# Moving the query and key transposes of three of sixteen head pairs of a routed-attention kernel from TensorE to VectorE, with earlier weights and a new plan for the placing DMAs

## The chip, the cores and the metric

The kernel runs on one core of one Trainium2 chip. The metric is the device time of one execution in microseconds (us). The profile is one execution, taken by the hardware profiler. PE is TensorE, PEld its weight loads, DVE is VectorE, ACT is ScalarE, POOL is GpSimd and SP is SyncE, which here does nothing but issue DMAs. Executions come with a state. Only fast ones are compared, unless a sentence says otherwise.

## The reference, cut to what matters

```python
q_n, k_n, c_n = (each row divided by its norm)          # shortened
q_assign = argmax(einsum('bhsd,hcd->bhsc', q_n, c_n))   # 16 clusters per head
k_assign = argmax(einsum('bhsd,hcd->bhsc', k_n, c_n))
mask = q_assign[..., :, None] == k_assign[..., None, :]
attn = softmax(where(mask, q @ k.T / 8, -1e9))          # 4 x 8 heads, 768 x 768
x = (attn @ v) laid out as 3072 tokens x 512
h = x @ w_in                                            # 512 x 2048
g = h + sin(alpha * h)**2 / (alpha + 1e-9)
out = g @ w_out                                         # 2048 x 512
```

The batch has four members. For each of them the kernel runs an attention stage (8 heads as 4 *pairs*, 12 *steps* for a pair, 48 in all) and then a feed-forward stage, FF. Pairs are numbered 0 to 15 and steps 0 to 191. One step computes a 128x768 block of scores on TensorE, its exponential on ScalarE, and six value products on TensorE for an earlier block.

## The kernel before: the parts that the change touches

A pair's q and k come in with positions on the partitions and must be turned, so that the head dimension lies there. The kernel has two ways for it. By TensorE, three 128x128 transposes into PSUM and a copy make one of four groups:

```python
def prep_T(m, g, bk=None, eng="dve"):
    ...
    for jj in range(NJ2):
        nc.tensor.transpose(out=bk[:, P*jj : P*jj + P], in_=src[:, h, P*jj : P*jj + P], identity=ident_f)
    nc.vector.tensor_scalar_mul(out=s["T32"][:, g, :], in0=bk[:, 0:HS], scalar1=1.0 / QDIV)
```

By VectorE, a transpose within 32x32 blocks goes to `Tq`, and eight DMAs on SP then put the blocks in their places in `T32`:

```python
def prep_D(m, g):
    ...
    nc.vector.transpose(out=s["Tq"][:, g, :], in_=src[:, h, :].rearrange("p (j e d) -> p e j d", e=2, d=32))

def prep_S(m):                       # "the placing"
    s["T32"] = trp.tile([P, 4, HS], F32, tag="T32", name="T32")
    for i in range(4):
        for e in range(2):
            lo = D * (i // 2) + 32 * e
            nc.sync.dma_start(out=s["T32"][lo : lo + 32, :, QS*(i%2) : QS*(i%2) + QS],
                              in_=s["Tq"][32*i : 32*i + 32, :, QS*e : QS*e + QS])
```

From `T32` come three things: casts on POOL into `QK`, the operand of the scores; the *cluster products* (`prep_asn`, four matmuls against the centroids); and from these, by four VectorE pieces (`prep_hot`), one-hot *rows* that four more DMAs on SP carry into `QK` (`prep_move`), where they mask the scores. TensorE takes its instructions in order, so a cluster product whose `T32` is not there holds back the scores of every later step.

Before, pairs 2 to 7 went by TensorE and pairs 8 to 15 by VectorE. A dictionary of steps says when each piece is put into its engine's order:

```python
first = {1: 0, 2: 4, 3: 12, 4: 20, 5: 28, 6: 36}          # pairs 2..7: transposes at s0..s0+3,
...                                                       # casts s0+2, s0+4, products s0+5
at(s0 - 5 + g, lambda g=g: prep_D(m, g))                  # pairs 8..: transposes, then
at(s0 - 2, lambda: prep_S(m))                             # the placing, products 19 steps later
```

Loads of q, k, v and of the feed-forward weights are issued by POOL, in POOL's order. "Load at step n" names a place in that order, not a time. In attention 1 to 3 each free step also takes a *fill*, one output product of the batch member before.

The softmax here doesn't subtract the row's maximum and nothing guards it: scores larger than these inputs give would overflow.

## Time and profile before

The time is 326.79 us (median of four executions, 325.74 to 328.09). The profiled one has a span of 325.0 us. Stages, by the starts of the exponentials in the timeline of ScalarE (attention: from the first exponential of a stage to its last; FF: from there to the next stage's first, or to the end):

| | start | attn 0 | FF 0 | attn 1 | FF 1 | attn 2 | FF 2 | attn 3 | FF 3 and end |
|---|---|---|---|---|---|---|---|---|---|
| before, us | 14.09 | 43.62 | 31.96 | 41.34 | 31.81 | 41.63 | 31.58 | 39.44 | 49.52 |

How to read it: 47 step distances of attention at ScalarE's own pace, 0.71 to 0.74 each, would be some 34 us. What is above that is TensorE work that doesn't fit under an exponential, or a wait. This is the summary line of the chain that ended last, from the page of the kernel before:

```profile
PE 70%; ACT 10%; DVE 9%; issue 5%; POOL 3%; DMA 2%; SPq 1%; ACTq 0%; DVEq 0%; POOLq 0%
```

and this is what TensorE waited for in attention 0 (engine, line, what for; us in total, times, longest):

```profile
PE S L313 <- ACT pT L319: 1.2, 5, 0.3
PE OB L328 <- DVE xs L340: 0.6, 2, 0.5
PE S L313 <- POOL QK L185: 0.5, 1, 0.5
```

TensorE carries 70% of the chain and DMAs only 2%. From 14.1 us on, the first scores apart, no wait in attention 0 is longer than 0.5 us, and none is for a DMA.

### The profile page before, as it was taken

Reading aid. Unit: us, or ns where it says so; the run is one execution under the profiler, and the core shown is the slowest. Engines: PE = TensorE matmul, PEld = TensorE weight load, DVE = VectorE, ACT = ScalarE, POOL = GpSimd, SP = SyncE. Lnnn points to the kernel's source line nnn. Section 1 sums busy time; section 2 is a strip of 40 time slices with the busy share of each in tenths; the row PEclk is TensorE's granted clock in tenths of the full one; section 3 lists DMA queues with packets and bytes.
Section 4 is the critical chain, followed back from the end, with each engine's and each line's share of the span. In section 5 each row is a group of like instructions: output and inputs, shape, how many; then the busy total and the mean of one; then the engine's idle time right before and its main releaser. Section 6 shows DMA issues by size and latency. Waiting matters only on the chain.

```text
span 325.0 us, 7163 instructions
## 1 busy us (share of the span) xinstructions
PE 306.9 (94%) x2744; PEld 183.3 (56%) x2787; DVE 206.1 (63%) x361; ACT 241.7 (74%) x325; POOL 112.6 (35%) x175
## 2 busy tenths in 40 slices
PE   6699999899999999999999999999999999999995
PEld 3276666555555665555556565555556566555544
DVE  4468888387837566677837766677836522577721
ACT  5388888787778988787678888787778999687300
POOL 7848797620017089530005476430006200000000
PEclk9989999999999999999999999999999999999999
DMA  7455398993016959550043858520043200000031
GB/s 228 139 189 162 123 217 187 216 206 118 2 65 198 242 129 248 199 177 2 0 125 97 235 114 245 130 81 2 0 114 96 61 35 34 0 35 0 0 126 70
DMA packets 26290, 37.78 MB, mean 116 GB/s; under 512 B 3880, under 2 KB 20112, under 8 KB 26256
## 3 DMA queue, kind: packets, MB, share of 16 engines
q0 software_dynamic: 8704, 19.93, 23.8%
q1 hardware_dynamic: 17312, 17.33, 19.3%
q8 instruction: 22, 0.36, 0.5%
q14 instruction: 12, 0.10, 0.1%
q10 hardware_dynamic: 240, 0.06, 0.1%
HBM read 27.30 MB, written 6.29 MB: 103 GB/s over the span
## 4 chain that ended last, share of the span: by engine, by line
PE 70%; ACT 10%; DVE 9%; issue 5%; POOL 3%; DMA 2%; SPq 1%; ACTq 0%; DVEq 0%; POOLq 0%
PE S L389 17%; PE M L360 13%; PE S L313 9%; ACT pT L319 8%; PE M L389 8%; PE OB L328 6%; PE OB L360 4%; PE S L314 4%; PE M L211 3%; PE S L360 2%; POOL QK L185 1%; SPq L175 1%; DVE Tq L164 1%; PE M L352 1%; PE M L143 1%
## 5 line engine op out<-in xcount | busy, mean ns | idle before, releaser
L319 ACT ACTIVATE pT<-S 128x768 bf16<-128x768 f32 x192 | 145.3, 810 | 27.1 <-PE S L314 24.8
L360 PE MATMUL M<-w_out_bf,gT 128*128 128x512 bf16 (+1 forms) x259 | 82.1, 372 | 0.6 <-DVE asT L243 0.3
L313 PE MATMUL S<-QK 81*128 81x512 bf16 x192 | 73.7, 384 | 6.5 <-DMA QK<-ohT 2.3
L389 PEld LDWEIGHTS <-w_in_bf 128*128 128x128 bf16 x512 | 49.6, 98 | 39.0 <-issue 3.1
L328 PEld LDWEIGHTS <-pT 128*128 128x128 bf16 x1152 | 56.0, 98 | 24.2 <-DVE xs L340 3.0
L389 PE MATMUL S<-xT,w_in_bf 128*128 128x512 bf16 (+1 forms) x348 | 65.0, 325 | 1.4 <-DVE gT L409 0.8
L190 POOL TENSOR_SCALAR QK<-T 64x384 bf16<-64x384 f32 x64 | 33.3, 520 | 92.5 <-DMA T<-Tq 78.6
L328 PE MATMUL OB<-VX,pT 128*128 128x65 bf16 x1152 | 61.2, 194 | 1.4 <-DVE xs L340 1.4
L400 ACT ACTIVATE s_sb<-S,alpha_col 128x768 bf16<-128x768 f32 x44 | 39.4, 902 | 24.2 <-PE S L389 14.2
L360 PEld LDWEIGHTS <-gT 128*128 128x128 bf16 x400 | 39.0, 98 | 27.2 <-issue 1.0
L314 PE MATMUL S<-QK 81*128 81x256 bf16 x192 | 52.4, 273 | 0.0
L409 DVE SCALAR_TENSOR_TENSOR gT<-u_sb,ralpha,S 128x768 bf16<-128x768 bf16 x44 | 44.5, 1013 | 11.4 <-ACT u_sb L405 8.1
L185 POOL CAST QK<-T 64x768 bf16<-64x768 f32 x32 | 26.6, 830 | 45.1 <-DVE T L149 39.1
L314 PEld LDWEIGHTS <-QK 81*128 81x128 bf16 x192 | 18.9, 99 | 22.2 <-issue 7.7
L389 PE MATMUL M<-xT,w_in_bf 128*128 128x512 bf16 (+1 forms) x156 | 29.7, 324 | 0.7 <-DVE gT L409 0.5
L407 DVE TENSOR_TENSOR u_sb<-s_sb 128x768 bf16<-128x768 bf16 x40 | 23.1, 577 | 7.8 <-ACT s_sb L400 7.8
L339 DVE RECIPROCAL rec<-OB 128x6 f32<-128x6 f32 x32 | 6.0, 187 | 34.4 <-PE OB L328 34.4
L313 PEld LDWEIGHTS <-QK 81*128 81x128 bf16 x192 | 18.8, 98 | 15.0 <-issue 10.8
L409 DVE SCALAR_TENSOR_TENSOR gT<-u_sb,ralpha,M 128x512 bf16<-128x512 bf16 (+1 forms) x40 | 22.8, 611 | 6.4 <-ACT u_sb L405 6.0
L400 ACT ACTIVATE s_sb<-M,alpha_col 128x512 bf16<-128x512 f32 (+1 forms) x40 | 20.9, 574 | 7.4 <-PE M L389 7.4
L360 PE MATMUL OB<-w_out_bf,gT 128*128 128x512 bf16 (+1 forms) x76 | 24.6, 357 | 0.0
L405 ACT ACTIVATE u_sb<-s_sb 128x768 bf16<-128x768 bf16 x24 | 20.2, 843 | 0.8
(82 smaller groups left out, 261.6 us busy)
## 6 DMA issues: line engine op xcount, KB each, us to landing
T<-Tq SPq DMA_DIRECT2D x64, 96.0 KB, 3.4
out_dram<-o_sb SPq DMA_DIRECT2D x23, 256.0 KB, 2.1
v<-in_v_dram POOLq DMA_DIRECT2D x14, 384.0 KB, 4.5
q<-in_q_dram POOLq DMA_DIRECT2D x13, 384.0 KB, 5.1
k<-in_k_dram POOLq DMA_DIRECT2D x13, 384.0 KB, 6.2
w_in_bf<-in_moe_w_in_dram POOLq DMA_DIRECT2D x4, 512.0 KB, 8.0
w_out_bf<-in_moe_w_out_dram POOLq DMA_DIRECT2D x4, 512.0 KB, 11.1
QK<-ohT SPq DMA_DIRECT2D x60, 24.0 KB, 4.3
```

The lines of the kernel that those rows point to most:

```text
L185: nc.gpsimd.tensor_copy(out=QK[0:D, m % NQK, h, :, HS * par : HS * par + HS], in_=src)
L190: nc.gpsimd.tensor_scalar(out=QK[0:D, m % NQK, h, t].rearrange("c (n i a) -> c i n a", i=4, a=32)[:, 2 * par : 2 * par + 2], in0=src[:, t] ...
L313: nc.tensor.matmul(out=dst[:, 0:512], lhsT=lhsT, rhs=T[:, 0, 0:512], start=True, stop=True)
L314: nc.tensor.matmul(out=dst[:, 512:S], lhsT=lhsT, rhs=T[:, 0, 512:S], start=True, stop=True)
L319: nc.scalar.activation(out=pT, in_=area(i)[:, 0:S], func=ACTF.Exp, scale=escale)
L328: nc.tensor.matmul(out=o3[:, j, :], lhsT=pT[:, P * j : P * j + P], rhs=VX[m % NVX][:, h, jof(m // NHP, kt), :], start=(kt == 0 and j == 0) ...
L360: nc.tensor.matmul(out=bk[:, lo:hi], lhsT=gT[:, f, P * mt : P * mt + P], rhs=w_out_bf[:, f, lo:hi], start=(f == 0), stop=(f == NF - 1),)
L389: nc.tensor.matmul(out=ar[lo // 512][:, 0 : hi - lo] if isinstance(ar, tuple) else ar[:, lo:hi], lhsT=lhsT, rhs=xT[:, kk, lo:hi], start=(k ...
L400: nc.scalar.activation(out=s_sb[:, lo:hi], in_=src, func=ACTF.Sin, scale=alpha_col[:, f : f + 1])
L405: nc.scalar.activation(out=u_sb, in_=s_sb, func=ACTF.Square)
L407: nc.vector.tensor_tensor(out=u_sb, in0=s_sb, in1=s_sb, op=ALU.mult)
L409: nc.vector.scalar_tensor_tensor(out=gT[:, f, lo:hi], in0=u_sb[:, lo:hi], scalar=ralpha[:, f : f + 1], in1=src, op0=ALU.mult, op1=ALU.add,)
```

## The change

The intent is to take transposes off TensorE, which sets the pace of attention, and give them to VectorE and DMAs, which have room. Pairs 4, 5 and 6 go by `prep_D`, as all from 8 do. The DMA side gets three `T32` buffers instead of two. From a placing to its products the plan now has 14 or 15 steps for pairs 4 to 6 and 16 for pairs from 8 on; placings and products of pairs from 8 on stand some 8 to 11 steps earlier in the plan. Weights are loaded from step 1 on, so that they are out of the way of feed-forward 0, where the loads of pairs 8 to 10 now come. The core of the diff (cut are the `MIX` cases, which fit pair 7's layout to its neighbours, pair 7's fourth transposing group in feed-forward 0, the loads of pairs 8 to 10 there, and an earlier place for `alpha`):

```diff
-    NPE = 2 * NHP
+    NPE = NHP
+    MIX = NHP + 3
-    trp = ctx.enter_context(tc.tile_pool(name="trp", bufs=2))
+    trp = ctx.enter_context(tc.tile_pool(name="trp", bufs=3))
...
+    def hot_steps(m, a):
+        asn_at.add(a)
+        if 1 < a < ASTEPS:
+            at(a - 1, lambda: prep_asn(m, 0, 2))
+            at(a, lambda: (prep_asn(m, 1, 2), prep_hot(m, 0)))
+        else:
+            at(a, lambda: (prep_asn(m), prep_hot(m, 0)))
+        at(a + 1, lambda: prep_hot(m, 1))
+        at(a + 2, lambda: prep_hot(m, 2))
+        at(a + 3, lambda: (prep_hot(m, 3), prep_move(m)))
...
+    plan_of = {                    # transposes, casts, products
+        1: ((), (), 1, prep_T),
+        2: ((6, 7, 8, 9), (8, 10), 12, prep_T),
+        3: ((14, 15, 16, 17), (16, 18), 20, prep_T),
+        4: ((10, 11, 16, 17), (30, 31), 32, prep_D),
+        5: ((21, 22, 24, 25), (38, 39), 40, prep_D),
+        6: ((33, 34, 36, 37), (49, 50), 51, prep_D),
+        7: ((), (52, 54), 56, prep_T),
+        8: ((48, 49, 50, 52), (65, 66), 68, prep_D),
+    }
+    for m in range(9, NP):
+        k0 = STEPS * (m - 3)
+        plan_of[m] = (tuple(k0 + d for d in (-12, -11, -9, -8)), (k0 + 5, k0 + 6), k0 + 8, prep_D)
...
+    for m, i in {3: 0, 4: 0, 5: 10, 6: 18, 7: 26, 11: 56, 12: 66, 13: 95, 14: 95, 15: 95}.items():
+        at(i, lambda m=m: load_qk(m, eng=nc.gpsimd))
...
-            at(max(0, STEPS * m - 14), lambda m=m: load_v(m, nc.gpsimd))
+            at({2: 2, 3: 12, 4: 24, 5: 36}.get(m, STEPS * m - 26), lambda m=m: load_v(m, nc.gpsimd))
...
-        (23, load_w_in, 0), (30, load_w_out, 0), (36, load_w_in, 1), (42, load_w_in, 2), ...
+        (1, load_w_in, 0), (9, load_w_out, 0), (19, load_w_in, 1), (27, load_w_in, 2), (35, load_w_out, 1), ...
...
-            if fill and r % STEPS != 7:
+            if fill and i not in asn_at:
```

## The prediction

> **What bounds the kernel now.** I first split the span at the change of the ScalarE function (exponential in attention, sine in the feed-forward part), because the page's whole-span shares mix eight stages with different limits. This is the view of stretches, for attention 0, feed-forward 0, attention 1 and attention 2: length, then busy time of PE, weight loads, DVE, ACT and POOL, granted clock, DMA share, GB/s.
>
> ```profile
> 14.10:58.50 44.40, 41.60 (x500) 28.20 (x500) 33.91 (x64) 37.09 (x48) 33.86 (x44) 0.96 0.66 174
> 58.50:89.70 31.20, 29.70 (x184) 17.00 (x186) 23.40 (x34) 23.22 (x34) 5.56 (x8) 1.00 0.65 125
> 89.70:131.80 42.10, 40.54 (x463) 24.89 (x471) 25.31 (x51) 36.17 (x48) 22.84 (x36) 1.00 0.69 183
> ...
> 162.80:205.30 42.50, 41.09 (x469) 24.71 (x477) 27.43 (x54) 36.01 (x50) 20.96 (x36) 1.00 0.64 164
> ```
>
> PE looks full everywhere. The skill's page "Perfetto Trace Analysis", section "Identifying the Most-Contended Engine", says that matmul busy time misjudges headroom because matmuls are pipelined; the trace agrees: attention 1 shows 463 matmuls of 0.19 to 0.5 us in 40.5 us, far more than fit end to end. So I took the second view, the timeline of PE, and read starts, not durations.
>
> ```profile
> 18.89 0.35 PE L328 MATMUL OB<-VX,pT 128*128 128x65 bf16 x6
> 19.07 0.52 PE L143 MATMUL M<-ident_f,k 128*128 128x128 f32 x3
> 19.43 0.38 PE L313 MATMUL S<-QK 81*128 81x512 bf16 x1
> 19.65 0.27 PE L314 MATMUL S<-QK 81*128 81x256 bf16 x1
> 19.76 0.35 PE L328 MATMUL OB<-VX,pT 128*128 128x65 bf16 x6
> ```
> ```profile
> 116.68 0.35 PE L328 MATMUL OB<-VX,pT 128*128 128x65 bf16 x6
> 116.95 0.85 PE L211 MATMUL M<-T,cnB 128*32 128x384 f32 x8
> 117.74 0.39 PE L313 MATMUL S<-QK 81*128 81x512 bf16 x1
> 117.96 0.27 PE L314 MATMUL S<-QK 81*128 81x256 bf16 x1
> 118.07 0.38 PE L360 MATMUL M<-w_out_bf,gT 128*128 128x512 bf16 x1
> ```
>
> From starts, PE needs 0.33 us for the scores of a step, 0.18 for its six value products, 0.36 for three transposes (19.07 to 19.43), 0.79 for one pair's cluster products (116.95 to 117.74), and 0.22 for one output product that fills a step. ScalarE in turn ran eight exponentials in 5.89 us where nothing held it up, 0.736 each. A plain step (0.51, or 0.73 with a fill) therefore just fits under the exponential, and anything more is added to the time, since only two score areas exist. The distances between successive exponential starts show it: 0.71 to 0.74 in plain steps, 0.87 in transposing steps (0.33+0.18+0.36), 1.40 in cluster steps of attention 1 to 3, 1.06 with the transposes of the finished x (six), about 0.91 where two value groups and a fill meet.
>
> **What the Trainium skill says of the parts.** "VectorE: DVE Perf Modes", section "The three transpose paths": the TensorE transpose goes to PSUM, the VectorE one stays in SBUF but only turns 32x32 blocks. Both are in this trace: TensorE path 0.36 us of PE plus a VectorE copy of 545 ns per group; VectorE path 535 ns for the same 128x384 elements, then a DMA that places the blocks. So VectorE pays about the same and the bill moves from PE to DMA. "DMA: Bandwidth & Descriptors", section "Issuing engines are not separate DMA queues", says that transfers from all engines share the same 16 DMA engines and interleave. The trace agrees: a QK<-ohT issued at 49.8 landed at 56.25, with the weight piece issued at 48.4 (56.24), 6.5 us, against 1.9 to 2.5 us when nothing was ahead of it.
>
> **The change, part by part.** The group list of attention 0:
>
> ```profile
> L211 PE MATMUL M<-T,cnB 128*32 128x384 f32 x48 | 5.2, 509 | 0.0
> L143 PE MATMUL M<-ident_f,k 128*128 128x128 f32 x30 | 5.2, 283 | 0.0
> L143 PE MATMUL M<-ident_f,q 128*128 128x128 f32 x30 | 5.2, 282 | 0.0
> ```
>
> 60 transposes are 20 steps of three (pairs 2 to 6). Pairs 4, 5 and 6 leave PE: 12 steps. Those twelve (20 to 23, 28 to 31, 36 to 39) lasted 0.71+1.68+0.87+0.87, 1.20+0.87+0.87+0.87 and 0.87+0.87+0.71+1.34 = 11.7 us. Without transposes I give them 0.72, 0.71 in a step without value products, 0.88 in a double one and 0.84 with x's transposes: about 9.1. **Saved: 2.7.**
>
> Cluster products are halved into two steps (192 columns, 0.39 each). Five of six whole ones cost 0.57, 0.67, 0.34, 0.56 and 0.67 over their step = 2.8; the sixth, pair 1's in step 1, stays whole. Of four halved ones a half costs 0.51+0.39-0.73 = 0.17 beside single value products and nothing in a step without them; pair 5's halves fall on a double step (+0.2) and on x's transposes (+0.4). Sum about 1.3; pair 6 goes to attention 1. **Saved: 1.5.**
>
> Attention 1: pair 6's halves come in (+0.4), the last three transposes of pair 7 go out (1.09 to 0.73, -0.36). A halved pair here has one half with a fill (0.51+0.22+0.39 = 1.12 against 0.73) and the other in a step without value products (0.33+0.39 = 0.72), so +0.4 with what the next double step loses, against about 0.6 net before: -0.2 each for three pairs, +0.4 for a pair more. One step of 1.48 (step 63), where four VectorE transposes back to back held up the normalisation that the value products need, should become 0.91 because the four are now spread over five steps and the one-hot work over four: -0.6. Two late steps (1.07 and 0.98) to plain: -0.4. **Saved: 1.1.** Attention 2: four pairs, -0.8; steps 111 and 112 (1.46, 1.34) to 0.91 and 1.06, -0.8; step 139 (1.74) loses its extra 0.34. **Saved: 1.9.** Attention 3: one cluster pair of two leaves (-0.5), the other is halved (-0.2), step 157 of 1.02 becomes plain (-0.3). **Saved: 1.0.** Three more fills fit into attention 3 (47 for 44) and leave the PE-bound feed-forward 3: 3 x 0.22 = **0.65**. The fourth transposing group of pair 7 enters feed-forward 0: **+0.36**.
>
> VectorE: 12 copies of 545 ns against 12 transposes of 535: nothing. POOL casts change from four of 830 ns to eight of 520 per pair, +0.84 us for three pairs, unimportant unless POOL stalls. The weights save nothing directly: no wait on w_in or w_out appears before feed-forward 0; moving them only clears DMA time there for the loads of pairs 8 to 10.
>
> Sum: 2.7+1.5+1.1+1.9+1.0+0.65-0.36 = **8.5 us**, to 318.3, if every transfer comes in time.
>
> **What DMA takes back.** This list says what the transfers weigh:
>
> ```profile
> T<-Tq SPq DMA_DIRECT2D x64, 96.0 KB, 3.4
> ...
> w_in_bf<-in_moe_w_in_dram POOLq DMA_DIRECT2D x4, 512.0 KB, 8.0
> w_out_bf<-in_moe_w_out_dram POOLq DMA_DIRECT2D x4, 512.0 KB, 11.1
> ```
>
> From landings one behind the other: q or k 1.0 us each, v about 1.1, a weight piece 2.3 to 3.5; a pair's placing is 1024 packets of 768 B at some 60 ns over 16 engines, 3.8 us. By estimate from these, attention 0 must move by step 39 five q/k pairs (10), five v (5.5), four or five weight pieces (12 to 15) and two placings (7.7): 35 to 38 us in about 32. In arrival order, pair 1's one-hot rows land near 25 to 26 us for step 12 at about 24.9; pair 4's placing near 40 to 41 for step 31 at about 40.4; pair 5's near 49 for step 39 at about 46.5. PE runs in order, so a late one stops the scores too. That walk gives up to 4 us. But POOL also waits for the placed tiles and then issues later loads later, weights need not be ahead in each ring, and steps as uneven as these look as if they had been set from traces. I take about 1.2 us.
>
> **Rivals.** (1) DMA saturates attention 0: the cluster products of pairs 4 and 5 wait for their tile and the time is 321.5 to 323. For it: 6 to 7 us landings in the second half of attention 0 already; against: slices at 0.3 to 0.5 DMA share up to 40 us, room that the early weights use. (2) VectorE becomes the bound at the start of attention 1 (one-hot of pairs 6 and 7, transposes of pair 8, stores: about 12 us of work in steps 48 to 59, some 12 us long): stalls in front of value products, 319.5 to 320.5. (3) ScalarE alone is the floor, so that all PE savings are lost: 326. Against it: 24.8 us of ScalarE idle before exponentials, ended by the scores.
>
> **Range and chances.** Without stalls 318.3, with the full walk 322.3; centre 319.6. The 2% line is 320.2, so it is close: faster 0.56, same 0.41, slower 0.03. Range 316.3 to 323.2.
>
> **What would show it.** Right: attention 0 about 40 us long, no 0.87 steps after step 17, cluster steps of 1.1 and 0.7 rather than 1.4 and 0.7, attention 2 near 40.5, feed-forward stages within 0.5 us of now, except the last, shorter by 0.6. Wrong: idle PE before the cluster products released by T<-Tq, idle before scores of step 12 released by QK<-ohT, or value products waiting for VectorE early in attention 1.

## The result, and the profile after

The changed kernel takes 337.56 us (median of four executions, 334.37 to 339.72; the longest is slow and counts for nothing further; the median of the three fast ones is 336.93). The ratio to the kernel before is 1.0295, with a 95% interval of 1.0208 to 1.0382: it is slower. Here and below a ratio is the mean time of one kernel's fast runs over that of the other's in the same rounds, so it is not quite the ratio of the medians quoted. The predicted range ended at 323.2.

The chain that ended last, on the page of the changed kernel:

```profile
PE 75%; DMA 8%; DVE 7%; ACT 6%; issue 2%; SPq 0%; DVEq 0%; ACTq 0%
```

DMAs went from 2% to 8% of a span of 336.3 us, that is from some 6 to some 27 us. The view of stretches, for attention 0, attention 1 and attention 2 (length, busy time of PE, weight loads, DVE, ACT, POOL, granted clock, DMA share, GB/s):

```profile
14.10:65.30 51.20, 41.31 (x490) 26.55 (x490) 30.43 (x60) 36.58 (x48) 36.31 (x53) 0.90 0.97 230
...
96.80:144.80 48.00, 43.01 (x477) 25.38 (x485) 31.65 (x59) 36.46 (x49) 23.69 (x39) 0.96 0.67 168
...
175.70:216.90 41.20, 40.61 (x470) 24.38 (x476) 28.87 (x55) 36.28 (x49) 25.95 (x44) 1.00 0.67 161
```

Read the first line beside its partner in the prediction (44.40 us). PE is busy as long as before, but now for 41.31 of 51.20 us. The DMA share went from 0.66 to 0.97, and the granted clock from 0.96 to 0.90. Attention 1 is longer too, by 6 us; attention 2 is a little shorter. By the starts of exponentials:

| us | start | attn 0 | FF 0 | attn 1 | FF 1 | attn 2 | FF 2 | attn 3 | FF 3 and end |
|---|---|---|---|---|---|---|---|---|---|
| after | 14.37 | 50.16 | 32.28 | 47.14 | 31.79 | 40.37 | 31.84 | 39.22 | 49.09 |
| less before | +0.3 | +6.5 | +0.3 | +5.8 | 0.0 | -1.3 | +0.3 | -0.2 | -0.4 |

The differences sum to 11.3 us, the difference of the spans. What TensorE waited for in attention 0, and below the line of dots in attention 1:

```profile
PE M L220 <- DMA T<-Tq: 4.8, 1, 4.8
PE S L326 <- DMA QK<-ohT: 1.8, 1, 1.8
...
PE M L220 <- DMA QK<-ohT: 3.0, 1, 3.0
```

Each is a single wait. L220 are the cluster products, L326 the scores. The 3.0 us are put down to pair 8's rows, which SP issued just behind pair 9's placing. The products don't read rows but the placed tile: its eight placings were issued from 115.70 to 120.29, and the last of them landed at 127.94. TensorE's check of that DMA's semaphore ended at 128.02, and after three more such checks the products began at 128.40. So the placing ended this wait too, and the name that the view gives is that of a later DMA on the same semaphores. The timeline of PE shows the longest wait and what follows it:

```profile
50.33 0.54 PE L341 MATMUL OB<-VX,pT 128*128 128x65 bf16 x12
55.72 0.87 PE L220 MATMUL M<-T,cnB 128*32 128x192 f32 x8 [4.85 <-DMA T<-Tq]
56.52 0.61 PE L326 MATMUL S<-QK 81*128 81x512 bf16 x1
56.92 0.42 PE L327 MATMUL S<-QK 81*128 81x256 bf16 x1
```

TensorE stands still for 4.85 us, because the products of pair 5 need their placed tile. After that everything takes longer: the half of the products starts 0.80 us before the next scores (the whole took 0.79 before the change), and the 512-column scores matmul starts 0.40 us before its 256-column partner (0.22 before). The view of stretches says why, at the end of that wait and after it:

```profile
54.10:55.70 1.60, 0.00 (x0) 0.01 (x1) 0.00 (x0) 0.00 (x0) 0.91 (x2) 0.51 1.24 210
55.70:57.00 1.30, 1.28 (x10) 0.43 (x11) 0.00 (x0) 0.00 (x0) 0.00 (x0) 0.50 1.18 305
```

The clock is granted at half rate. In the clock records it is so from 26.8 us for 3.4 us (after the wait for the rows), from 54.1 for 6.8, and from 129.2 for 3.4 (after the wait in attention 1). The Trainium skill has this: "TensorE: Matmul & The Clock Gate", section "Part 1: The HAM clock gate", says that the clock is passed at half or full rate by activity in a free-running window of 3413 ns. The lengths agree: every such span inside attention, in all runs below, is one or several times 3.4 us.

Why was the tile so late? This is the chain from SP's side, for pair 3's rows and pair 5's placing, and then the timeline of SP (start, us, count):

```profile
39.65 6.85 DMA QK<-ohT
46.52 9.06 DMA T<-Tq
55.72 0.87 PE M L220 x8
```
```profile
39.05 2.94 SPq L300 DMA_DIRECT2D QK<-ohT  x4
42.15 6.25 SPq L176 DMA_DIRECT2D T<-Tq  x8
```

The third of pair 5's four transposes was done at 39.34 and the last at 40.50. SP first issued the four DMAs of pair 3's rows and then the eight placings, at 0.6 us each, the last at 47.80; the part of them that the first half needs had landed at 55.58. In this program a DMA of SP also waits for the eighth before it: placings started at 43.94, 44.99 and 46.52, and the eighth ones before them had landed at 43.92, 44.97 and 46.51. So SP is here a queue of eight, first in, first out, and one slow transfer delays all behind it. The eight are of this program's making: in the trace its SP DMAs take eight semaphores in turn. The transfers were slow, I take it, because a weight piece (issued at 39.97, landed at 55.2) and q and k of pair 7 (38.5 and 39.2, landed at 49.9 and 51.2) shared the engines; run 5 tests this. The plan had 14 steps from the placing to the first half of the products, and 15.2 us went by from the last transpose to that half.

### The profile page after: what moved, and what is told of

Its sections match the earlier page's. It is cut to its first block, busy times and chain, and to the rows that moved or that the text cites.

```text
span 336.3 us, 7215 instructions
## 1 busy us (share of the span) xinstructions
PE 309.3 (92%) x2741; PEld 182.9 (54%) x2783; DVE 205.9 (61%) x360; ACT 242.4 (72%) x326; POOL 116.4 (35%) x188
## 4 chain that ended last, share of the span: by engine, by line
PE 75%; DMA 8%; DVE 7%; ACT 6%; issue 2%; SPq 0%; DVEq 0%; ACTq 0%
PE S L402 15%; PE M L373 14%; PE S L326 12%; PE OB L341 8%; PE M L402 7%; DMA QK<-ohT 6%; PE S L327 5%; PE OB L373 4%; ACT pT L332 4%; PE M L220 4%; DMA T<-Tq 3%; PE S L373 2%; DVE gT L422 2%; PE M L144 2%; ACT s_sb L413 1%
## 5 line engine op out<-in xcount | busy, mean ns | idle before, releaser
L373 PE MATMUL M<-w_out_bf,gT 128*128 128x512 bf16 (+1 forms) x261 | 83.0, 373 | 0.2
L326 PE MATMUL S<-QK 81*128 81x512 bf16 x192 | 74.9, 391 | 8.4 <-DVE T L150 2.1
L341 PEld LDWEIGHTS <-pT 128*128 128x128 bf16 x1152 | 57.3, 99 | 22.8 <-issue 1.8
L402 PE MATMUL S<-xT,w_in_bf 128*128 128x256 bf16 (+1 forms) x345 | 64.8, 325 | 1.5 <-DVE gT L422 0.9
L341 PE MATMUL OB<-VX,pT 128*128 128x65 bf16 x1152 | 62.1, 196 | 0.2 <-DVE xs L353 0.2
L197 POOL TENSOR_SCALAR QK<-T 64x384 bf16<-64x384 f32 x88 | 46.8, 532 | 37.5 <-DMA T<-Tq 27.2
L413 ACT ACTIVATE s_sb<-S,alpha_col 128x768 bf16<-128x768 f32 x44 | 39.3, 900 | 23.9 <-PE S L402 13.8
L402 PE MATMUL M<-xT,w_in_bf 128*128 128x256 bf16 (+1 forms) x154 | 29.4, 324 | 0.3
L326 PEld LDWEIGHTS <-QK 81*128 81x128 bf16 x192 | 18.9, 98 | 15.5 <-issue 11.5
L373 PE MATMUL OB<-w_out_bf,gT 128*128 128x512 bf16 (+1 forms) x79 | 25.8, 357 | 0.0
L209 POOL CAST VX<-v 128x768 bf16<-128x768 f32 x16 | 13.2, 827 | 35.1 <-PE OB L341 34.2
L118 POOL DMA_DIRECT2D q<-in_q_dram x13 | 9.6, 736 | 42.1 <-DVE Tq L165 42.0
```

The costliest lines, as they stand in the source:

```text
L197: nc.gpsimd.tensor_scalar(out=QK[0:D, m % NQK, h, t].rearrange("c (n i a) -> c i n a", i=4, a=32)[:, 2 * par : 2 * par + 2], in0=src[:, t] ...
L209: nc.gpsimd.tensor_copy(out=VX[m % NVX][:, :, :, 0:D], in_=st[m]["v32"])
L326: nc.tensor.matmul(out=dst[:, 0:512], lhsT=lhsT, rhs=T[:, 0, 0:512], start=True, stop=True)
L341: nc.tensor.matmul(out=o3[:, j, :], lhsT=pT[:, P * j : P * j + P], rhs=VX[m % NVX][:, h, jof(m // NHP, kt), :], start=(kt == 0 and j == 0) ...
L373: nc.tensor.matmul(out=bk[:, lo:hi], lhsT=gT[:, f, P * mt : P * mt + P], rhs=w_out_bf[:, f, lo:hi], start=(f == 0), stop=(f == NF - 1),)
L402: nc.tensor.matmul(out=ar[lo // 512][:, 0 : hi - lo] if isinstance(ar, tuple) else ar[:, lo:hi], lhsT=lhsT, rhs=xT[:, kk, lo:hi], start=(k ...
```

## The experiments

Before the runs I had these theories: the placed tiles come late, because DMAs stand before them in SP's order or share the engines (which ones: weights, loads, the rows); what is lost is the wait and then the half clock; the rival was that the early weights alone are to blame, or that the plan of VectorE and TensorE is slow whatever the DMAs do. Letters in the recorded texts are working names of theories that those texts give in numbers. "Step 39" means the distance from exponential 39 to exponential 40. Of the expectations, those of runs 2, 6, 9 and 12 came true in the main; the others missed the time that their first theory gave. Waits, stages and steps are read from one profiled execution of each run, and fast executions of one program differ too (334.37 to 338.20 for the changed kernel), so a single wait can be off by a microsecond or more.

### 1. Weights at their old steps

```diff
-        (1, load_w_in, 0), (9, load_w_out, 0), (19, load_w_in, 1), (27, load_w_in, 2), ...
+        (23, load_w_in, 0), (30, load_w_out, 0), (36, load_w_in, 1), (42, load_w_in, 2), ...
```

> The changed kernel with the weight pieces back at the steps of the kernel before (23, 30, 36, 42, 47). Theory A (the early weight loads fill the DMA engines ahead of the one-hot rows and of the placed tiles, and PE, in order, waits for those): the wait before step 12 shrinks from 1.8 us to under 0.7 us, the 4.8 us wait before pair 5's cluster products falls to under 2 us, attention 0 falls from 51 us to 43 to 46, the time from 337.6 to 329 to 333. Rival B (the placing DMAs are late by themselves, whatever else runs): the 4.8 us wait stays above 4 us and the time within 1% of the changed kernel. The waits in attention 1 stay under both, since no weight is moving there.

Measured: 338.85 us, ratio 1.0369 (1.033 to 1.0407). Attention 0 takes 50.35 us, as with the change. The waits only moved: 2.21 us before step 12, 1.68 for pair 4, 2.53 for pair 5, 3.25 in attention 1. That the weights come early is not the cause; put late, other pieces of them meet the same placings.

### 2. Pairs 4 to 6 back on TensorE

```diff
-    NPE = NHP
-    MIX = NHP + 3
+    NPE = 2 * NHP
+    MIX = -1
-        4: ((10, 11, 16, 17), (30, 31), 32, prep_D),
+        4: ((20, 21, 22, 23), (22, 24), 25, prep_T),       # 5 and 6 likewise
```

> The changed kernel with pairs 4 to 6 transposed by PE again at the steps of before; weights stay early. If the placings are needed for the overload (theory A: loads, early weights and placings together), no PE wait over 1 us is left in attention 0 except that before step 12, attention 0 is 43 to 45 us (PE pays 2.7 us again), and the time 328 to 332, what is left being attention 1. If the early weights alone did the harm, attention 0 stays above 47 us.

Measured: 329.21 us, ratio 1.0054 (1.001 to 1.0098). Attention 0 is 45.68 us instead of 50.16, so these three pairs are most of the loss there. A wait of 1.84 us for pair 1's rows before step 12 stays, and one of 1.97 us for a placed tile in attention 1 (45.25 us), with half clock for 3.4 us after it.

### 3. More steps between placing and products

```diff
-        4: (..., (30, 31), 32, prep_D),   5: (..., (38, 39), 40, prep_D)
+        4: (..., (34, 35), 36, prep_D),   5: (..., (44, 45), 46, prep_D)
+        x = 6 if m in (9, 10) else 0      # casts and products of 9 and 10 six steps later
```

> The changed kernel with the cluster products of pairs 4 and 5 four and six steps later and those of pairs 9 and 10 six steps later; all loads and placings unmoved. If the distance of 15 steps is what fails (PE in order meets a tile that is still under way), the waits for T<-Tq in attention 0 and the wait at step 80 fall to under 1 us in total, the half-clock stretches after them go too, and the time is 323 to 328. If the DMA engines are so far behind that later steps wait as well, new waits of together over 3 us show up and the time stays above 332.

Measured: 333.38 us, ratio 1.0205 (1.0167 to 1.0243). The waits for placed tiles in attention 0 are gone, and attention 1 is 42.04 us. But the next thing in the queue came late: pair 3's rows, 2.10 us before step 36, and half clock of 6.8 us with it. In attention 2 a cast of v on POOL came late (1.71 us), because POOL's own order waits for the moved casts. More steps help; they don't make the queue shorter.

### 4. TensorE kept busy while it waits

```diff
+            if m == 5:
+                for _ in range(22):           # dummy products into a bank that is overwritten next
+                    nc.tensor.matmul(out=bk[:, 0:512], lhsT=warm[:, 0:P], rhs=warm[:, P:640], ...)
```

> The changed kernel with 22 useless matmuls of 512 columns (4.7 us at full clock) just before pair 5's cluster products, where PE sits idle for 4.8 us. Theory C (a wait is paid twice, because the granted clock falls to 0.5 for 6.8 us after it): the half-clock stretch after that wait is gone from the clock record and the time is 1.5 to 3 us shorter than the changed kernel's although work was added. Rival (the clock falls for another reason, for example DMA load): the half-clock stretch stays and the time is the same or longer.

Measured: 341.18 us, ratio 1.0403 (1.0342 to 1.0465). After pair 5's wait there is no half clock, and step 40 takes 1.41 us where it took 2.52: the clock's part, 1.1 us in that step, is shown. The expectation for the time missed, since in this run pair 4, whose plan was untouched, waited 3.74 us (0.80 in the changed kernel's profile), with 6.8 us of half clock. Pair 9's wait is longer too, 4.04 us against 2.96. (One of the four executions, 347.49, is slow.) How late a placing is can differ by microseconds between two programs that have the same plan for it.

### 5. Loads taken out of the placings' way

```diff
-    {3: 0, 4: 0, 5: 10, 6: 18, 7: 26, 11: 56, 12: 66, ...}     # q and k
+    {3: 0, 4: 4, 5: 10, 6: 20, 7: 34, 11: 56, 12: 82, ...}
-    weights at 1, 9, 19, 27, 35, 40, 44
+    weights at 7, 12, 33, 41, 44, 47, 47
```

> The changed kernel with nothing altered but the steps of loads: q and k of pair 4 at step 4 instead of 0, pair 6 at 20, pair 7 at 34, pair 12 at 82 instead of 66; weight pieces at 7, 12, 33, 41, 44 and 47, so that no weight piece and no load of pair 7 is issued while pairs 4 and 5 are being placed. Theory A' (what counts is what is in the DMA engines at the same time as a placing, whichever weight piece it is; the run with late weights only swapped which piece that was): the wait before step 12 falls under 0.7 us, the waits before the cluster products of pairs 4, 5 and 9 to under 1 us each, no half-clock stretch after 20 us, attention 0 is 40 to 43 us, attention 1 41 to 42 us, the time 318 to 324. Rival B' (the queue that issues the placings, 0.6 us each and never more than eight under way, sets their landing): pair 5 still waits 2.5 us or more, the time stays above 328.

Measured: 331.37 us, ratio 1.0163 (1.0106 to 1.0219). With only the places of loads changed, attention 0 went from 50.16 to 46.05 us and attention 1 from 47.14 to 43.03. The waits for pair 5 and for pair 9 are gone (none in attention 1 above 0.94 us). The one for pair 4 (2.19 us) and the one before step 12 (2.48 us, with another of 0.7 in the total) are there, each with 3.4 us of half clock:

```profile
PE S L326 <- DMA QK<-ohT: 3.2, 2, 2.5
...
PE M L220 <- issue: 2.2, 1, 2.2
```

The part of pair 5's placing that the first half needs landed 7.3 us after SP's first issue of it, where it took 13.4 in the changed kernel; TensorE also came to it later, at 54.5 us instead of 50.9, so the wait's end is not the loads' doing alone. What shares the engines with a placing matters, then, and not only the transposes on VectorE. But the time missed the expected 318 to 324, so loads are not all of it.

### 6. Sixteen placings of half the size

```diff
-                nc.sync.dma_start(out=s["T32"][lo : lo + 32, :, ...], in_=s["Tq"][32*i : 32*i + 32, :, ...])
+                for gg in range(0, 4, 2):
+                    nc.sync.dma_start(out=s["T32"][lo : lo + 32, gg : gg + 2, ...], in_=s["Tq"][..., gg : gg + 2, ...])
```

> The changed kernel with each pair's placing cut into 16 DMAs of 48 KB instead of 8 of 96 KB: the same bytes and packets, twice the issues. Rival B' (issue and the limit of eight under way): each pair's placing takes 4.8 us longer or more, the waits in attention 0 grow by at least 5 us in all, new waits for the placed tile appear in attention 1 and 2, the time is above 345. Theory A' (bytes in the DMA engines): the waits grow by less than 2 us and the time stays within 1.5% of the changed kernel's.

Measured: 363.65 us, ratio 1.1142 (1.1081 to 1.1203). The bytes are the same. The waits for placed tiles are 7.02 (pair 4), 6.40 (5), 6.11 (9), 1.22 (10), 2.24 (12) and 2.13 us (13), and 31 us of half clock go with them. The lists of DMA issues of the changed kernel and of this one (count, size, median us from issue to landing):

```profile
T<-Tq SPq DMA_DIRECT2D x88, 96.0 KB, 4.3
```
```profile
T<-Tq SPq DMA_DIRECT2D x176, 48.0 KB, 3.0
```

One DMA of half the size lands sooner, yet a placing is later by microseconds, because sixteen issues stand in a queue of eight (its last issue comes 9.9 to 11.9 us after its first for pairs 4 to 6, against 4.6 to 6.0 in the changed kernel). The number of issues is a cost of its own.

### 7. Attention 0 as before, in the new order

This has pairs 4 to 6 on TensorE (as in 2), weights and early loads as before the change, and the rest of the new plan (pairs 2 and 3 later, v earlier); load 12 at step 82.

> Attention 0 as in the kernel before (pairs 4 to 6 on PE, loads and weights at the old steps), but the rest as changed (three T32 buffers, 15 steps for pairs 8 on, loads of pairs 8 to 10 in feed-forward 0, one-hot work over four steps), with pair 12's load at step 82. If the later stages of the changed kernel are sound by themselves, attention 1 to 3 take 40 to 41.5 us each, no wait over 1 us before cluster products, and the time is 322 to 325. If 15 steps are too few also there, pair 9 waits again for 2 us or more and the time is 326 or more.

Measured: 329.63 us, ratio 1.0086 (1.0037 to 1.0136). No wait for a placed tile above 0.9 us; attention 1 to 3 take 41.89, 40.65 and 39.01 us. Attention 0 takes 47.04 all the same: pair 1's rows let TensorE wait 2.45 us before step 12. So that wait needs neither the early weights nor pairs 4 to 6 on VectorE (run 9 shows that early weights can make one too).

### 8. The first loads behind a cast

```diff
-    q and k of pair 4 at 0, v of pair 2 at 2, first weights at 1
+    all three at step 8, behind pair 2's first cast in POOL's order; pair 4's first transposes at 12, 13; load 5 at 11
```

> The changed kernel with the loads of pair 4, the second v and the first weight piece moved behind pair 2's first cast in the GpSimd queue (step 8), and pair 4's first two VectorE transposes at steps 12 and 13; nothing else. Theory D (a load's step is only its place in the GpSimd queue; with no cast in front of them that waits for VectorE, the loads of steps 0 to 2 are all issued at once and pair 1's one-hot rows land behind them): the wait before step 12 falls from 1.8 us to under 0.5, its half-clock stretch goes, step 11 is 1.0 us or less instead of 2.8, the time is 2 to 4 us below the changed kernel's, the waits for pairs 5 and 9 staying as they are. Rival: the rows are late because they are issued one step later than before (step 4 for step 3): the wait stays above 1.3 us.

Measured: 341.16 us, ratio 1.0457 (1.0404 to 1.0511). Step 11 takes 0.94 us, as in the kernel before: the first loads, issued at once by an idle POOL, were what made pair 1's rows late. But now VectorE waits for pair 4's data in the transposes planned for step 12, and later for pair 5's, and value products wait for VectorE (1.33 and 1.94 us); half clock ran for 23.9 us without a break. Attention 0 took 54.95 us. One wait was traded for a worse one.

### 9. The kernel before with early weights

```diff
-        (23, load_w_in, 0), (30, load_w_out, 0), (36, load_w_in, 1), ...   # kernel before
+        (1, load_w_in, 0), (9, load_w_out, 0), (19, load_w_in, 1), ...
```

> The kernel before with the weight pieces at the steps of the change (1, 9, 19, 27, 35, 40, 44, 47) and nothing else. If early weights do harm only through the placings, the kernel before, which has none in attention 0, stays within 1% (324 to 330). If they do harm by themselves, there is a wait of over 1 us before step 12 or later one-hot rows, and the time is 330 or more.

Measured: 326.75 us, ratio 1.002 (0.9997 to 1.0043). Alone, this part of the change costs nothing that can be seen in the time, though it does bring a wait of 1.72 us before step 12.

### 10. Only the later stages of the change

Attention 0 exactly as before; later stages as changed, with pair 7's products at step 62 and load 12 at step 82.

> Attention 0 exactly in the order of the kernel before (transposes, casts, whole cluster products, one-hot work in three steps, loads and weights), the stages after it as in the changed kernel, with pair 7's cluster products at step 62 and pair 12's load at step 82. From the stages of earlier runs: attention 0 44.4 as before, attention 1 40 to 41, attention 2 41, attention 3 40, feed-forward 3 shorter by 0.6: 321.5 to 324, faster than the kernel before by 1 to 1.5%. If the new wait of e7 at step 12 shows here too, it is not the order of the loads that makes it.

Measured: 329.76 us, ratio 1.0105 (1.0055 to 1.0156). One wait is left: 2.57 us before pair 10's products in attention 1 (44.89 us), then 3.4 us of half clock. Load 12, which I had moved there in run 5, was under way beside that placing (issued at 118.3 and 119.1, the placing from 117.6 on). The view names rows, which SP issued behind the placing:

```profile
PE M L220 <- DMA QK<-ohT: 2.6, 1, 2.6
```

### 11. Products far behind the placings

Pairs 4 to 6 by VectorE, as changed, with products at steps 44, 50 and 56, weights and loads late, and the casts of v moved.

> Pairs 4, 5 and 6 by VectorE transposes as in the change, but with their cluster products at steps 44, 50 and 56, those of pair 7 at 62, pair 4's placing at step 22, pair 5's at 31, pair 6's at 40, one-hot rows of pairs 1 to 3 and the loads in the order of before. If the distance between placing and products was the cause, no PE wait for a placed tile over 0.5 us is left in attention 0, attention 0 is 40 to 42 us, attention 1 41 to 43, the time 319 to 323, under the kernel before and under b1. If VectorE cannot carry six one-hot works in attention 1, that stage is 44 or more.

Measured: 348.56 us, ratio 1.0688, and **the result was wrong** (relative error 0.073). I didn't find why. Its time settles nothing: it has waits of 5.56 us for q of pair 7, a load that I had put too late, of 5.92 for rows before step 60, and of 4.72 for VectorE as feed-forward 1 begins, whose causes I did not follow. In its attention 0 (41.79 us), no wait was for a placed tile.

### 12. The later stages, with load 12 at step 95

```diff
-    {..., 11: 56, 12: 82, 13: 95, ...}      # of run 10
+    {..., 11: 56, 12: 95, 13: 95, ...}
```

> The kernel of the run with the later stages only, with one load moved: q and k of pair 12 are asked for at step 95, with those of pairs 13 to 15, instead of step 82, where they stood in front of pair 10's placing DMAs. Theory (the placing DMAs are late because others stand before them in a first-in, first-out order, and not because fifteen steps are too few): the wait of 2.57 us before pair 10's products and the half clock after it go; steps 92 to 94, which took 4.18, 1.73 and 1.16 us, take 1.2, 0.9 and 0.75, so some 4.2 us come off the profiled span of 326.0, which makes 321.5 to 322.5, and a time of 323 to 325.5, a ratio of 0.988 to 0.997 to the kernel before: the only version so far that is ahead of it. Rival (fifteen steps are too few by themselves when FF weights are not the cause): the wait stays above 1.5 us and the ratio at 1.005 to 1.012.

Measured in five rounds: 324.56 us (323.16 to 326.7) against 327.77 for the kernel before, ratio 0.991 (0.9862 to 0.9957). The wait before pair 10's products is gone with one number changed. Its stretches of attention 1, attention 2 and attention 3:

```profile
88.80:129.50 40.70, 40.53 (x475) 24.10 (x474) 28.04 (x55) 35.61 (x48) 17.69 (x31) 1.00 0.62 151
...
161.10:201.70 40.60, 40.32 (x473) 23.95 (x472) 28.11 (x55) 35.48 (x48) 25.05 (x43) 1.00 0.66 159
...
233.30:273.00 39.70, 39.48 (x456) 24.40 (x455) 13.04 (x27) 35.98 (x48) 0.83 (x1) 1.00 0.11 38
```

PE is busy for nearly all of each, at full clock. This version beats the kernel before, though by less than 2%. The profiled spans differ by 3.6 us (321.4 against 325.0). Of that 1.2 us are chance: the kernel before ran steps 1 to 4 at half clock (4.35 us, here 3.14), which its other runs need not do. The later stages give the rest: feed-forward 0 +0.3, attention 1 -0.65, feed-forward 1 -0.2, attention 2 -1.0, attention 3 -0.4, the end -0.4.

### 13. The same, with pairs 4 to 6 on VectorE and room for them

```diff
-        4: ((20, 21, 22, 23), (22, 24), 25, prep_T),       # of run 12
-        5: ((28, 29, 30, 31), (30, 32), 33, prep_T),
-        6: ((36, 37, 38, 39), (38, 40), 41, prep_T),
+        4: ((18, 19, 21, 22), (34, 36), 38, prep_D),
+        5: ((27, 28, 30, 31), (44, 45), 47, prep_D),
+        6: ((36, 37, 39, 40), (52, 53), 55, prep_D),       # 7: casts at 57, 58 instead of 52, 54
```

> The same kernel as the last, but pairs 4 to 6 go by VectorE transposes again, with 16 steps from the last transpose to the products (22 to 38, 31 to 47, 39 to 55) and no loads in front that were not there before the change. Theory: the work that the change takes off TensorE in attention 0 is real, and only the waits and the half clock ate it; then no wait above 1 us before the products of pairs 4 to 6, steps 24 to 47 take 18.5 to 19 us instead of 20.5, and the profiled span is 1.5 to 3 us below that of the kernel with pairs 4 to 6 on TensorE: a time of 321 to 323.5. Rival: with three placings in 40 steps the queue is too slow whatever the plan, so waits of over 1.5 us come back before products or before step 12, 24 or 36, with half clock after them, and the time is 326 or more. The result is not sure to be right: the run that set these products furthest back was wrong, and its cause isn't known; the plan of value tiles and loads that this one doesn't share with it would then be cleared of it.

Measured in five rounds, beside run 12: 329.73 us, ratio 1.0054 (1.0006 to 1.0102). The result is right. In attention 0 no product waits for its tile by more than 0.23 us, but it takes 43.77 us against run 12's 42.27. A transpose of pair 4 stands in VectorE's order in front of the normalization that the value products of step 21 need; TensorE waits 0.92 us, and half clock begins and lasts 10.2 us. The expectation missed. Pair 10 also waits 2.01 us here, with a plan for it that made no wait in run 12.

### 14. Transposes off the normalization

```diff
-        4: ((18, 19, 21, 22), (34, 36), 38, prep_D),   6: ((36, 37, 39, 40), ...)
+        4: ((21, 22, 23, 24), (36, 37), 38, prep_D),   6: ((39, 40, 41, 42), ...)   # 5: 28 to 31
```

> The kernel of the run with room for pairs 4 to 6, with the transposes of pairs 4 and 6 three and one to three steps later (21 to 24, 28 to 31, 39 to 42), so that none stands in VectorE's order before the normalization of step 20 to 21, after pair 3's one-hot pieces. In that run a wait of only 0.92 us for the normalization began a half clock of 10.2 us, and attention 0 was 1.5 us longer from step 0 to step 47 (43.8 against 42.3) than with pairs 4 to 6 on TensorE. Theory (the saving is real, and lost to the half clock alone): no half clock in attention 0, steps 24 to 47 in 18.5 to 19.3 us instead of 20.5, steps 0 to 47 in 40 to 41, and a time of 321 to 324 if pair 10 doesn't wait, 3 us more if it does. Rival (TensorE's share is by then so low in those steps that other waits and the half clock come anyway, and ScalarE or VectorE sets the step): steps 0 to 47 in 42 us or more, half clock in attention 0 again.

Measured: 330.93 us, ratio 1.0118 (1.0069 to 1.0167). There is no half clock at that place any more. But pair 4's products now wait 5.67 us for their tile, and 6.8 us of half clock go with that wait.

### 15. The wait of run 13 filled

```diff
+            if i == 21:                        # in front of the waiting value products
+                for _ in range(6):
+                    nc.tensor.matmul(out=bk[:, 0:512], lhsT=warm[:, 0:P], rhs=warm[:, P:640], ...)
```

> The kernel of the run with room for pairs 4 to 6, with six dummy matmuls of 512 columns (1.3 us) in TensorE's order just in front of the value products that waited 0.92 us for the normalization in step 21; nothing else is changed, the dummies write a bank that nobody reads then. Theory (that wait sets off the half clock, which then costs some 3 us): the 10.2 us of half clock from 33.8 are gone, step 21 is 0.2 to 0.5 us longer, steps 22 to 35 some 2.5 us shorter, and the time 2 to 3 us less than the sibling's, 326.5 to 328. Rival (the half clock comes from the low share of TensorE's work in those steps and not from the one wait): a half clock of 6.8 us or more still begins between step 21 and step 30.

Measured: 329.67 us, ratio 1.0059 (1.0018 to 1.01). The 10.2 us of half clock are gone by six dummy products alone, as expected. The time isn't shorter, which was not expected, and the steps tell why. Steps 24 to 37 (14 of them) take:

| kernel | 24 to 37, us | then |
|---|---|---|
| run 12, pairs 4 to 6 on TensorE | 12.58 | no wait |
| run 13, half clock until 44.0 us | 12.62 | no wait |
| run 14, full clock | 10.51 | pair 4 waits 5.67 us |
| run 15, full clock | 10.52 | pair 4 waits 2.71 us |

With full clock nearly every step is at ScalarE's 0.71 to 0.74 us, and these steps are 2.06 us shorter than in run 12. Only half of that is the saving that the change was made for. The six steps that hold transposes in run 12 (28 to 31, 36 and 37) lose 1.11 us. The two that hold cluster products there (25 and 33) lose 1.09, but these products are put off, to steps 38 and 47, and not saved; step 24 takes 0.14 more. What is gained is lost at once, since TensorE reaches pair 4's products earlier (at 47.5 us in run 15, 50.05 in run 13) and the tile isn't (it landed at 50.15 and 50.19). Run 13 only had no wait because half clock held it back until the tile was there. In run 15, 6.8 us of half clock follow the wait of 2.71. The end of that chain in run 15 and its view of stretches:

```profile
37.16 0.59 SPq L300
37.75 0.05 issue
37.80 0.03 SPq L176
...
50.25 1.50 PE M L220 x8
```
```profile
38.00:42.00 4.00, 3.26 (x46) 2.32 (x46) 2.67 (x6) 3.81 (x6) 0.82 (x1) 1.00 1.07 215
42.00:46.00 4.00, 3.60 (x45) 2.35 (x45) 1.24 (x3) 4.00 (x6) 0.00 (x0) 1.00 1.15 208
46.00:50.00 4.00, 1.42 (x17) 0.71 (x15) 0.00 (x0) 2.43 (x4) 0.68 (x2) 0.86 1.00 214
```

SP reaches the placing at 37.8, behind pair 3's rows. The last of its eight DMAs was issued at 43.35, 0.02 us after the landing of the eighth before it, and landed at 50.15; the products began at 50.25. The DMA share is 1.0 and above from 38 to 50 us: weights and loads on POOL's queue fill the engines. That is the bound that takes the place of TensorE.

## Why the prediction was wrong

**The step that failed** is "I take about 1.2 us" for what DMA takes back. In attention 0 of the changed kernel single waits alone sum to 7.5 us (1.83 before step 12, 0.80 for pair 4, 4.85 for pair 5), and in attention 1 one is 2.96. The mechanism was in the text, as rival 1 and in the walk, down to the three places. The size was not, for three reasons that the runs show.

- The walk counted a placing by its packets, 3.8 us, in order of arrival. It is also eight issues of 0.6 us in SP's order, behind four of the rows, in a queue of eight. The walk put pair 5's landing at 49; what the first half of the products needs landed at 55.58. Run 6 doubles the number of issues alone and loses 26 us more.
- The walk ended with attention 0. Attention 1 lost 5.8 us, most of it in the same way: pair 9's placing was under way beside q and k of pair 12 (issued at 117.3 and 118.1), with 16 steps to its products where the kernel before gave 19, which the prediction doesn't mention. (A wait of 0.94 us for VectorE, before pair 10's products, is not of this kind.) Moving loads alone brought back 4.1 us there (run 5), six more steps 5.1 (run 3).
- The argument "steps as uneven as these look as if they had been set from traces" was a hope, not a reading, and with two others (POOL's later loads, weights not always ahead) it pulled the number from the walk's 4 down to 1.2.

**Half clock** is a term that the sum lacked altogether. Compared with the undisturbed steps of the same shape, the changed kernel's steps 14 to 16 took 1.28, 1.77 and 1.20 us where the plan of run 1, at full clock, took 0.74, 1.05 and 1.20: some 1.3 us. Step 40 took 1.1 us more than in run 4, where TensorE was kept busy, and steps 81 and 82 in attention 1 took 1.73 and 1.22 where run 12 has 0.91 and 0.73, 1.3 more. So some 3.7 us by this estimate, less than the waits but not small.

**The saving in attention 0** (2.7 by the transposes and 1.5 by halves, less than DMA takes) was right in kind for the transposes and not far off in size: 1.11 us in six of the twelve steps (run 15 against 12), where the text has 2.7 for all. It was shown only where the tile came too late afterwards, so no correct run has had it in the total. The halves were not tested apart; pair 3's, which had no long wait, took 0.39 us over two plain steps in the changed kernel but 0.66 in run 1, against 0.69 for the whole before. As a sum, attention 0 grew by 6.5 us with 7.5 of waits and some 2.4 of half clock, so the rest of it shrank by 3.4, of which 1.2 are chance (the kernel before ran steps 1 to 4 at half clock): by this estimate some 2.2 us were saved there, and the text has 4.2.

**The later stages** were over-read. For attention 1, 2 and 3 and the end the text has 1.1, 1.9, 1.0 and 0.65; run 12, without a wait, has 0.65, 1.0, 0.4 and 0.4, and +0.3 in feed-forward 0 as predicted (0.36). One cause is a plain misreading: I counted halved products for all pairs, but the code halves them only before step 48. Later they stay whole, pair 6's too, and only move to a step without value products: three steps (79 to 81) take 0.73, 1.21 and 0.91 us in run 12, against 1.40, 0.71 and 0.75 before. That is even, not the -0.2 per pair of the text. What came as written are the single long steps: 63 fell from 1.48 to 0.91, and 139 to 141 from 3.20 to 2.86.

**The rivals.** DMA saturation was the right one, and "321.5 to 323" too small by 15 us. VectorE as a bound early in attention 1 didn't come: no wait of TensorE there was for it (the one of 0.94 us is late in the stage); it came in runs 8 and 13, where a transpose stood before a normalization. ScalarE's floor is reached in runs 14 and 15, but the savings above it were real. **The signs named.** Of the three signs of being wrong, two came: idle PE before products released by T<-Tq (4.8 us) and before step 12 released by QK<-ohT (1.8 us). The third, value products waiting for VectorE, didn't. Of the signs of being right, attention 2 (40.37 us) and the feed-forward stages came as written, and attention 0 (50.16 instead of about 40) did not.

**What stays open.** Why run 11 was wrong isn't known; runs 13 to 15 share most of its plan and are right. Which loads would have to go for attention 0 to keep its saving wasn't found: in runs 13 to 15 attention 0 is 1.5 to 4.1 us longer than with the three pairs on TensorE. Why half clock follows some waits and not others is not settled. Fewer, larger placings were not run, nor were placings or rows on another engine's queue, which would have put run 6's reading to the opposite test.

## What to carry to other kernels

Taking work off the busiest engine moves every deadline forward: a DMA with so many steps of lead has less time once the steps get shorter, so count its lead in microseconds after the change, and count its issues and what stands before it in the same queue, not only its bytes. An engine that runs in order pays for one late tile with everything behind it, and TensorE pays a second time in half clock. When a large change fails, keep the stages where the traces show no new wait: here they alone are 1% faster than the kernel before.

## What the Trainium skill lacked or had wrong

- "DMA: Bandwidth & Descriptors", section "Issuing engines are not separate DMA queues", says that issuing from several engines only saves the sequencer's time, which is usually small beside the transfer. For one DMA that holds (0.6 us, with a median of 4.3 from issue to landing), but not for eight in a row: SP took 6.25 us over pair 5's placings, 0.6 for each and the rest in waits for landings, and twice as many issues of half the size cost 26 us (363.65 against 337.56).
- No page that I read warns of a queue like the one of eight that this program's semaphores make of SP: placings began 0.01 to 0.02 us after the eighth DMA before them had landed (43.94 after 43.92, 46.52 after 46.51).
- "TensorE: Matmul & The Clock Gate", section "Part 1: The HAM clock gate", has the clock at half rate after an idle window of about 3.4 us; further on the page says, without a length, that frequent short idle times can also bring it down. In these runs much shorter waits were enough at times: 0.92 us (run 13, then 10.2 us of half clock) and 1.83 us (the changed kernel, then 3.4 us), while waits of 1.84 us (run 2) and 1.72 us (run 9) had none after them. The lengths of the half-clock spans, 3.4, 6.8 and 10.2 us, agree with the page.
- No page that I read says what it costs to put the 32x32 blocks of VectorE's transposes in their places: 15.2 us from the last transpose to the product at the changed kernel's longest wait (40.50 to 55.72), while no product in attention 0 of the kernel before, where all tiles came by TensorE, waited for its tile.
